# Row sums made row-major and transposed by the DMA, in an H3 convolution beside a Strassen feed-forward

## The chip, the cores and the metric

One Trainium2 chip, one NeuronCore of it. The metric is the device time of one execution in microseconds (us). The kernel before has a median of 1271.46 us over three runs.

## The reference

A gated H3 convolution and a feed-forward are added to x; shapes are S = 2048 rows, D = 1024 columns, F = 3584 hidden columns, all in float32.

```python
x = q                                     # 1 x 2048 x 1024
xn = layernorm(x)
k_shift = sum(k_pad[:, t:t + S] * shift_k[:, 3 - t] for t in range(4))
kv = k_shift * v
y = irfft(rfft(kv, 2 * S) * rfft(ssm_k, 2 * S))[:, :S] + kv * ssm_D   # a long causal convolution per channel
out = x + xn * y + silu(xn @ w1) @ w2
```

For this document the last term matters: the rows of x are layer-normed, multiplied by w1 (GEMM1), put through SiLU and multiplied by w2 (GEMM2). The convolution runs beside it as background work on VectorE and ScalarE, with some matmuls for its Fourier transforms, and is added into the same output.

## The kernel before, in words

**Precision.** Each operand is split into a high and a low float16 part (`split`, L357: the high part by an ACT copy, the low part by a DVE scalar_tensor_tensor). Each product is three matmuls, high by high, high by low, low by high: lines 917 to 919 in GEMM1 (`steps`, L912), 1047 to 1049 in GEMM2 (`steps2`, L1043). [...]

**Seven products.** Most of GEMM1 is done in units of seven products in place of eight (Strassen in Winograd's form, `PRODUCTS`, L39). x is cut into quarters A11, A12, A21, A22 and their sums S1 to S4; each product takes one of the seven x tiles (A11, S3, S2, A12, S1, S4, A22 for P1, P7, P6, P2, P5, P3, P4) and one factor of w1. `units` (L953) writes the order: P1, P7, P6, P2, P5, the next unit's P1, P3, P4. Three products share the bank `two`: `evacuate` (L880) copies P1 on ACT into it, P6 is added onto it, ACT copies that out, P5 is added, ACT copies it out, P3 is added. `seen["P1"]`, `seen["P6"]` and `seen["P5"]` are set by these ACT copies, `made[...]` by the products. P2 is added onto P1's own bank `one`. The first four units are plain (eight products, `plain_unit`, L922; they need A11 and A12 alone). Then come 26 units with seven products: 12 for the upper 1024 rows (sp = 0), then 14 for the lower 1024 rows (sp = 1).

**Where the x tiles come from.** Rows arrive in 16 blocks t of 128 rows (`load_row`, L463), are normed on DVE (`ln_rows`, L469, the last step at L506), and transposed on PE through an identity (`transposes`, L512, matmuls at L525): each block in two groups of four 128x128 float32 transposes, 128 in all, into PSUM. Blocks 0 to 3 give A11 and A12 (`first_rows`, L533), and ACT keeps a copy of their transposes (`keep`, L548). Blocks 4 to 7 give A21 and A22; `lower_sums` (L575) and `upper_sums` (L590) make S1 to S4 from the transposed tiles on DVE (v_tt, L336), ACT copying A21 out of PSUM for it. All results are split into tiles of 128 x 4 x 4 x 2 x 128 float16, one megabyte each, in `places`. For sp = 1 (blocks 8 to 15) the same is done in background, with the split parts stored to DRAM (`spill`, L648, 28 stores of 256 KB into xspA and xspS). `load_x` (L990) brings the seven tiles back, one plain DMA of 1 MB each, as each place comes free: a place is free after its product in the last unit of sp = 0.

**Order of the work.** All engines run instruction lists that a planner writes at build time (`Order`, L106). Every stream of work is a Python generator with a bias; the planner takes the operation that can start first by its own costs (`V`, `A`, `T`, `L`, `X`, `G`, L313 to L331), less the bias. SP issues plain DMAs (L, L324) and DMA transposes (X, L329); the planner counts 0.4 and 0.6 us of SP for them and the same transfer time per byte for both. POOL issues the accumulating stores into `out` (G, L333). What the planner wrote is fixed: on the chip each engine takes its list in order and waits where it must. The existing DMA transposes are those of the convolution, hl<-cm, 128x1024 float16, 32 in all.

**GEMM2.** Plain row blocks t take five chunks of W2 each; `TOGETHER` (L1040) says which blocks share a pass over the chunks at its start, so that a chunk is used by several blocks before the next is needed. While a chunk is made, spare PSUM banks (`ff`) go to the convolution. Then `units2` (L1065) does seven-product units for the rest, with `evacuate2` (L1112) writing to `out`; in the last unit the quarter (1, 0) is not accumulated by POOL but loaded from `out` (hf<-out), added on DVE and stored by SP. "conv out" is the flag that the convolution's stores are issued.

**The convolution's end.** `rest` makes the gated result yt by DVE in tiles of its own ring or of `hts`, and POOL adds it to `out` once `copies` (L1186) has written x into that part of `out`.

Of the kernel before, what the change touches and what calls it, by code (L numbers as in the profile page):

```python
# [20 lines left out]
P = 128  # L21
# [267 lines left out]
def h3_ffn_kernel(ctx, tc, x, kp, vs, fs, shift, dskip, w1, w2, cfwd, cinv, out):  # L289
# [123 lines left out]
    sums_r = Ring(order, lnp, "s", 4)  # L413
    s1_r = Ring(order, lnp, "s1", 4)
    xst_r = Ring(order, lnp, "xst", 3)
# [47 lines left out]
    def load_row(t):  # L463
        yield xts_r.ready
        xts[t] = xns[t] = xts_r.tile([P, D], uses=6 if t < 4 else 2)
        yield L(xts[t][0], xr[t // T2, t % T2])
        flag["xt", t].set()

    def ln_rows():  # L469
        for t0, n, bias in ((0, 2, 0.26), (2, 2, 0.17), (4, 4, 0.15), (8, 8, 0.03)):  # L470
# [33 lines left out]
            for t in order_in:  # L504
                xt, i = xts[t][0], slice(t - t0, t - t0 + 1)
                yield V(lambda: nc.vector.tensor_scalar(xt, xt, m[:, 0, i], rstd[:, t:t + 1], op0=ADD, op1=MUL),  # L506
                        xt, [xt, m[:, 0, i], rstd[:, t:t + 1]], us=0.78)
                flag["xn", t].set()
# [3 lines left out]
    def transposes():  # L512
        jobs = [(t, a) for t in range(4) for a in range(2)]
        jobs += [(4 + i, a) for i in range(4) for a in range(2)]
        for i in range(4):
            jobs += [(12 + i, 0), (12 + i, 1), (8 + i, 0), (8 + i, 1)]
        for t, a in jobs:
            yield flag["xn", t]
            xn, tok = xns[t]
            yield ft.ready  # L520
            pt, ptok = ft.tile([P, KH, P], uses=2)

            def mm():
                for c in range(KH):
                    nc.tensor.transpose(pt[:, c, :], xn[:, (KH * a + c) * P:(KH * a + c + 1) * P], ident)  # L525
            yield T(mm, pt, [xn], 0.5, m=0.3)
            tok.set()
            pts.append((pt, ptok))
# [4 lines left out]
    def first_rows():  # L533
        for n, name in enumerate(("A11", "A12")):
            xo[0][name], xtok[0][name] = places[XPLACE[name]].tile([P, 4, KH, 2, P], F16)
        for t in range(4):
            two = []
            for name in ("A11", "A12"):
                yield next_pt
                two.append(pts.pop(0))  # L540
                pt, tok = two[-1]
                o = xo[0][name]
                add(split(o[:, t, :, 0], o[:, t, :, 1], pt, XS, (tok, flag["rows", t], flag["x", 0, name])), 0.2)
            add(keep(t, two), 0.19)

    kept = {}

    def keep(t, two):  # L548

        xt, xtk = xts[t]  # L550
        kept[t] = []
        for a, (pt, tok) in enumerate(two):
            o = xt[:, a * W:(a + 1) * W].rearrange("p (k w) -> p k w", k=KH)
            yield a_act(o, pt, AF.Copy)
            tok.set()
            kept[t].append((o, xtk))
        flag["kept", t].set()

    def next_sum(ring, uses):
        yield ring.ready  # L560
        return ring.tile([P, KH, P], uses=uses)

    def next_transposed():
        yield next_pt
        return pts.pop(0)

    def give(to, name, src, tok):

        put = to(name)
        if put is None:  # L570
            tok.set()
        else:
            add(put(src, tok), to.bias)

    def lower_sums(to, ring):  # L575

        a21, k21 = yield from next_transposed()
        c21, kc = yield from next_sum(sums_r, 1)
        yield a_act(c21, a21, AF.Copy)
        k21.set()  # L580
        give(to, "A21", a21, k21)
        a22, k22 = yield from next_transposed()
        s1, ks1 = yield from next_sum(ring, 2)
        yield v_tt(s1, a22, c21, ADD)
        k22.set()
        give(to, "A22", a22, k22)
        give(to, "S1", s1, ks1)
        return c21, kc, s1, ks1

    def upper_sums(to, ring, c21, kc, s1, ks1, t=None):  # L590

        if t is not None:
            yield flag["kept", t]
        a11, k11 = kept[t][0] if t is not None else (yield from next_transposed())
        s2, ks2 = yield from next_sum(ring, 2)
        yield v_tt(s2, s1, a11, SUB)
        ks1.set()
        give(to, "S2", s2, ks2)
        yield v_tt(c21, a11, c21, SUB)
        k11.set()  # L600
        give(to, "A11", a11, k11)
        give(to, "S3", c21, kc)
        a12, k12 = kept[t][1] if t is not None else (yield from next_transposed())
        s4, ks4 = yield from next_sum(ring, 1)
        yield v_tt(s4, a12, s2, SUB)
        ks2.set()
        k12.set()
        give(to, "A12", a12, k12)
        give(to, "S4", s4, ks4)

    second = {}

    def x_rows():
        yield from first_rows()
        second["A21"], second["tok"] = places[4].tile([P, 4, KH, 2, P], F16)
        for name in ("A22", "S2", "S3", "S1", "S4"):
# [4 lines left out]
        class Kept:  # L621
            bias = 0.14

            def __init__(self, i):
                self.i = i

            def __call__(self, name):
                if name in ("A11", "A12"):
                    return None
                o = (second["A21"] if name == "A21" else xo[0][name])[:, self.i]  # L630
                return lambda src, tok: split(o[:, :, 0], o[:, :, 1], src, XS, (tok, flag["x", 0, name]))

        yield 0.14
        half = []
        for i in range(4):
            half.append((yield from lower_sums(Kept(i), s1_r)))
        Kept.bias = 0.11
        yield 0.11
        for i in range(4):
            yield from upper_sums(Kept(i), xst_r, *half[i], t=i)  # L640

        class Spilled(Kept):
            bias = 0.02

            def __call__(self, name):
                return None if name == "A21" else lambda src, tok: spill(xsp[name][:, self.i], src, tok)

        def spill(o, src, tok):  # L648
            yield lambda: s1_r.ready() or xst_r.ready()
            r = s1_r if s1_r.ready() else xst_r  # L650
            st, stok = r.tile([P, KH, 2, P], F16)
            yield from split(st[:, :, 0], st[:, :, 1], src, XS, (tok,))
            yield L(o, st)
            stok.set()
            flag["spilled"].set()

        yield 0.02
        for i in range(4):
            part = yield from lower_sums(Spilled(i), sums_r)
            yield from upper_sums(Spilled(i), sums_r, *part)  # L660
        flag["x done"].set()

# [290 lines left out]
    def units():  # L953
# [5 lines left out]
        for n, (i, sp) in enumerate(todo):  # L959
# [8 lines left out]
            add(evacuate(i, 2 * sp, one, c, made, seen), EB)  # L968
            yield from product("P7", i, sp, c[0], True)
# [70 lines left out]
    TOGETHER = ([range(2)] + [(t,) for t in range(2, NT)],  # L1040
# [71 lines left out]
    def evacuate2(u, one, c, made, seen):  # L1112
# [16 lines left out]
        a, at_ = vs_r.tile([P, W])  # L1129
        yield made["P6"]  # L1130
# [13 lines left out]
        if last:  # L1144
            yield flag["conv out"]
            yield hfs.ready
            o, otok = hfs.tile([P, W])
            yield L(o, at(u, 1, 0))
# [12 lines left out]
    flag["conv out"] = Token(NG * 4 * 2)  # L1161
# [9 lines left out]
    def load_h():  # L1171
# [7 lines left out]
        for u, n in uses2():  # L1179
# [4 lines left out]
            flag["h2", u, n].set()  # L1184

    def copies():  # L1186
        n = NT // 2
        for a in range(NT):
            yield flag["unit", a // 2] if a < n else flag["result", a - n]
# [134 lines left out]
    def convolution(floor):  # L1324
# [368 lines left out]
        def gated(g, t, py, tok):  # L1693
# [3 lines left out]
            yield lambda: r.ready() or flag["quads", 1]() and hts.ready()  # L1697
            yt, ytok = (r if r.ready() else hts).tile([P, 2, 2, P], uses=2)
# [8 lines left out]
            for b in range(2):  # L1707
                yield G(out4[b][:, :, t, g * P:(g + 1) * P], yt[:, b])
                ytok.set()
                flag["conv out"].set()  # L1710
# [25 lines left out]
    def more_rows():  # L1736
        for t in (8, 9, 12, 13, 10, 11, 14, 15):
            yield from load_row(t)
        yield L(taps, shift)
        yield L(cfw, cfwd)  # L1740
        yield L(civ, cinv)

    def more_pairs():
        for n in range(2, len(pairs)):
            yield from load_pair(n)
            if n == 3:
                add(load_factors_late(), 0.05)

# [69 lines left out]
```

## Time and profile before

| | |
|---|---|
| median of three runs | 1271.46 us (1269.89 to 1276.68) |
| profiled execution: time, span | 1272.2 us, 1270.4 us |
| granted PE clock, mean | 0.992 |
| first GEMM matmul (L917) starts | 14.8 us |
| GEMM1 ends, GEMM2 begins | 595.7, 601.8 us |
| last GEMM matmul starts | 1259.83 us |
| packets, those under 512 B | 253894, 48752 |

How to read it. The page groups instructions by source line, engine, operation and tile names with the buffer numbers left out. A group row ends in its busy time and mean length (ns), then the idle time before it and what released it. A timeline row is start, length, engine, line, operation. A 128x512 matmul shows 0.38 us from its first to its last element, but the next one starts 0.215 us after it: matmuls overlap, and what counts is the distance between starts. DMA shares are those of 16 engines; a share at or over 1 means that they were full. "q" behind an engine's name is its queue: SPq rows are DMA issues, and their length is how long the issue held SP.

### The profile page before, as it was taken

The numbers are of one execution on the slowest core, as the hardware profiler recorded it, in microseconds if no ns is written. First come the engines' busy times: TensorE is split into PE (matmuls) and PEld (weight loads), VectorE is DVE, ScalarE is ACT, GpSimd is POOL, SyncE is SP. The second block draws the span as 40 slices with busy tenths as digits, with TensorE's granted clock in tenths as the row PEclk, the third lists the DMA queues.
The fourth block names the chain that finished last, engine by engine and source line by source line (L and its number), as shares of the span: only waits on it lengthen the run. The fifth ranks groups of instructions, "written<-read, shape, count | busy, mean of one in ns | idle before, by whom it ended". The sixth has DMA issues, their size and how long they took to land.

```text
span 1270.4 us, 17081 instructions
## 1 busy us (share of the span) xinstructions
PE 1234.8 (97%) x6018; PEld 595.6 (47%) x6018; DVE 1150.0 (91%) x1533; ACT 734.2 (58%) x1169; POOL 132.9 (10%) x141
## 2 busy tenths in 40 slices
PE   7899999999999999999999999999999999999996
PEld 6444544444444444444344544444454454445443
DVE  8999998899599969999999799989979989998995
ACT  6857887778766686657654542473263245535232
POOL 0000000000000030001210210120030021113213
PEclk9899999999999999999999999999999999999998
DMA  9447799979999798879998786599577668978766
GB/s 331 158 141 241 261 319 317 299 254 353 299 362 286 236 272 284 239 218 260 334 367 212 166 243 142 138 254 268 126 163 214 140 150 243 259 151 152 158 121 92
DMA packets 253894, 292.94 MB, mean 231 GB/s; under 512 B 48752, under 2 KB 167536, under 8 KB 251632
## 3 DMA queue, kind: packets, MB, share of 16 engines
q1 hardware_dynamic: 227072, 266.93, 66.7%
q0 software_dynamic: 26736, 24.92, 15.0%
q8 instruction: 47, 0.77, 0.2%
q14 instruction: 39, 0.32, 0.1%
HBM read 193.22 MB, written 98.57 MB: 230 GB/s over the span
## 4 chain that ended last, share of the span: by engine, by line
PE 24%; DVE 19%; issue 8%; DMA 6%; ACT 2%; POOL 2%; SPq 0%; POOLq 0%; DVEq 0%; ACTq 0%
DVE spec L336 7%; PE ff L1048 7%; PE ff L1047 7%; PE ff L1049 7%; DVE tmp L336 3%; POOL out L333 2%; DVE ht L339 1%; DMA hf<-in_w 1%; DVE x L339 1%; DVE acc L339 1%; DMA kin<-in_kp 1%; DVE spec L339 1%; DMA out<-yt 1%; PE ps L1493 1%; PE ps L1495 1%
## 5 line engine op out<-in xcount | busy, mean ns | idle before, releaser
L1047 PE MATMUL ff<-x,wo 128*128 128x512 f16 x864 | 327.9, 380 | 2.7 <-ACT x L347 1.6
L1048 PE MATMUL ff<-x,wo 128*128 128x512 f16 x864 | 328.1, 380 | 1.3 <-DVE x L339 1.3
L1049 PE MATMUL ff<-x,wo 128*128 128x512 f16 x864 | 328.0, 380 | 0.0
L917 PE MATMUL ff<-x,wo 128*128 128x512 f16 (+1 forms) x808 | 304.6, 377 | 3.5 <-ACT hf L347 3.4
L918 PE MATMUL ff<-x,wo 128*128 128x512 f16 (+1 forms) x808 | 304.4, 377 | 2.5 <-DVE x L339 2.5
L919 PE MATMUL ff<-x,wo 128*128 128x512 f16 (+1 forms) x808 | 304.4, 377 | 0.4 <-DVE wo L339 0.4
L336 DVE TENSOR_TENSOR spec<-spec 128x512 f32<-128x512 f32 (+2 forms) x256 | 261.0, 1054 | 2.3
L1049 PEld LDWEIGHTS <-wo 128*128 128x128 f16 x864 | 84.6, 98 | 103.8 <-issue 2.1
L1048 PEld LDWEIGHTS <-wo 128*128 128x128 f16 x864 | 84.6, 98 | 103.5 <-issue 4.6
L1047 PEld LDWEIGHTS <-wo 128*128 128x128 f16 x864 | 85.6, 99 | 100.3 <-issue 0.6
L919 PEld LDWEIGHTS <-wo 128*128 128x128 f16 x808 | 79.4, 98 | 96.9 <-issue 4.1
L918 PEld LDWEIGHTS <-wo 128*128 128x128 f16 x808 | 79.5, 98 | 92.3 <-issue 5.7
L917 PEld LDWEIGHTS <-wo 128*128 128x128 f16 x808 | 80.9, 100 | 87.9 <-issue 1.1
L333 POOL DMA_DIRECT2D out<-yt x64 | 72.4, 1300 | 344.0 <-DVE yt L339 204.3
L347 ACT ACTIVATE hf<-ff,invc 128x512 f32<-128x512 f32 x64 | 43.7, 684 | 111.7 <-PE ff L1049 87.7
L333 POOL DMA_DIRECT2D out<-hf x63 | 56.6, 898 | 459.6 <-ACT hf L347 400.1
L336 DVE TENSOR_TENSOR tmp<-spec 128x2048 f32<-128x2048 f32 (+1 forms) x48 | 92.6, 1935 | 1.1
L347 ACT ACTIVATE spec<-spec 128x1024 bf16<-128x1024 f32 x32 | 33.8, 1058 | 89.3 <-DVE spec L336 89.3
L339 DVE SCALAR_TENSOR_TENSOR acc<-kin,taps,acc 128x1024 f32<-128x1024 f32 x48 | 61.6, 1283 | 15.0 <-ACT acc L347 14.4
L339 DVE SCALAR_TENSOR_TENSOR ht<-hf,wsc,ht 128x1024 f16<-128x1024 f32 (+1 forms) x56 | 67.4, 1204 | 6.7 <-ACT ht L347 6.6
L347 ACT ACTIVATE ht<-hf,wsc 128x1024 f16<-128x1024 f32 (+1 forms) x56 | 61.0, 1089 | 10.8 <-DMA hsfS<-ht 4.1
L347 ACT ACTIVATE spec<-ps 128x512 f32<-128x512 f32 x92 | 52.9, 590 | 17.3 <-PE ps L1495 14.3
(175 smaller groups left out, 1744.2 us busy)
## 6 DMA issues: line engine op xcount, KB each, us to landing
wo<-hs SPq DMA_DIRECT2D x160, 256.0 KB, 3.5
hs<-ht SPq DMA_DIRECT2D x80, 256.0 KB, 4.5
out<-hf POOLq DMA_DIRECT2D x63, 256.0 KB, 4.3
wraw<-in_w SPq DMA_DIRECT2D x31, 512.0 KB, 5.9
raw<-in_w SPq DMA_DIRECT2D x28, 512.0 KB, 5.8
kin<-in_kp SPq DMA_DIRECT2D x16, 704.0 KB, 6.0
xt<-in_x SPq DMA_DIRECT2D x16, 512.0 KB, 7.3
kf<-in_fs SPq DMA_DIRECT2D x8, 1024.0 KB, 5.6
```

The source lines that it names most:

```text
L333: return Op("POOL", 1.1, 3.0, lambda: nc.gpsimd.dma_start(o, i, accum_op=ADD), [i], [o], m, n)
L336: return V(lambda: nc.vector.tensor_tensor(o, a, b, op=op), o, [a, b], **k)
L339: return V(lambda: nc.vector.scalar_tensor_tensor(o, a, s, b, op0=op0, op1=op1), o, [a, b] + ([] if isinstance(s, float) else [s]), **k)
L347: nc.scalar.activation(o, i, func, scale=scale, **kw)
L917: nc.tensor.matmul(o, w[:, 0, k], xf[:, :, k, 0], start=first and k == 0, stop=False, **kw)
L918: nc.tensor.matmul(o, w[:, 0, k], xf[:, :, k, 1], start=False, stop=False, **kw)
L919: nc.tensor.matmul(o, w[:, 1, k], xf[:, :, k, 0], start=False, stop=last and k == KH - 1, **kw)
L1047: nc.tensor.matmul(po, hx[:, n, 0, :], wc[:, n, 0, :], start=first and n == 0, stop=False, **kw)
L1048: nc.tensor.matmul(po, hx[:, n, 0, :], wc[:, n, 1, :], start=False, stop=False, **kw)
L1049: nc.tensor.matmul(po, hx[:, n, 1, :], wc[:, n, 0, :], start=False, stop=last and n == 3, **kw)
L1493: nc.tensor.matmul(o, cf[:, 0], hi[i], start=i == 0, stop=False, **kw)
L1495: nc.tensor.matmul(o, cf[:, 1], hi[i], start=False, stop=True, **kw)
```

## The change

1. Blocks 8 to 15 are no longer transposed on PE; `transposes` has 16 groups in place of 32. The sums are made row-major on DVE, in place, on the normed rows (`low_sums`, `up_sums`; as many 128x512 operations as before), and split row-major into new tiles `s`. For sp = 0, S1 to S4 are brought into the x tiles by 16 DMA transposes of 256 KB from SBUF. For sp = 1 the split parts are stored row-major, and `load_x` reads them back by seven DMA transposes of 1 MB from DRAM. ACT's copies of kept transposes and of A21 are gone.
2. The last step of the layer norm of blocks 4 to 7 is done by ACT (Identity with scale and bias) and not by DVE.
3. The first seven-product unit has the order P1, P2, P7, P6, next P1, P5, P3, P4. P2 waits there for the ACT copy of P1; P3 stands directly behind P5.
4. In GEMM2 three row blocks share the first pass over W2's chunks, where two did.
5. The load of hf<-out in the last unit stands ahead of the copy after P6, "conv out" counts only the first half of the column groups, and yt may take tiles of `wo` once the hidden tiles are loaded.
6. The copies of x into the second half of `out` are issued four results later; three constants (taps, cfw, civ) are loaded after the sixth weight pair and not after the rows.

```diff
-        for t, a in jobs:
+        for t, a in [(t, a) for t in range(8) for a in range(2)]:
...
+                if n == 4:
+                    yield a_act(xt, xt, AF.Identity, rstd[:, t:t + 1], nmr[:, t:t + 1])
...
+    def row_parts(sp, i, names, src, tok):
+        n = len(names)
+        yield sums_r.ready if n == 1 else sums_r.pairs
+        o, otok = (sums_r.tile if n == 1 else sums_r.pair)([P, n * KH, 2, P], F16, n)
+        yield from split(o[:, :, 0], o[:, :, 1], src.rearrange("p (k w) -> p k w", w=P), XS, (tok,))
+        for f, name in enumerate(names):
+            q = o[:, f * KH:(f + 1) * KH]
+            if sp == 0:
+                yield X(xo[0][name][:, i].rearrange("p k h w -> p (k h) w"), q.rearrange("p k h w -> p (k h w)"))
+                flag["x", 0, name].set()
+            else:
+                yield L(xsp[name][:, i], q)
+                flag["spilled"].set()
+            otok.set()
...
+    def low_sums(sp, i, bias):
+        x, y, z, v = quarters(sp, i)
+        low, tok = xns[8 * sp + 4 + i]
+        yield v_tt(v, z, v, ADD)
+        yield v_tt(z, x, z, SUB)
+        add(row_parts(sp, i, ("S3", "S1"), low, tok), bias)
+
+    def up_sums(sp, i, bias):
+        x, y, z, v = quarters(sp, i)
+        up, tok = xns[8 * sp + i]
+        yield v_tt(x, v, x, SUB)
+        xns[8 * sp + 4 + i][1].set()
+        yield v_tt(y, y, x, SUB)
+        add(row_parts(sp, i, ("S2", "S4"), up, tok), bias)
...
+            if n == 0:
+                yield seen["P1"]
+                yield from product("P2", i, sp, one[0])
+                made["P2"].set()
             yield from product("P7", i, sp, c[0], True)
...
-            yield from product("P2", i, sp, one[0])
-            made["P2"].set()
-            yield seen["P6"]
-            yield from product("P5", i, sp, two)
-            made["P5"].set()
+            if n > 0:
+                yield from product("P2", i, sp, one[0])
+                made["P2"].set()
+                yield seen["P6"]
+                yield from product("P5", i, sp, two)
+                made["P5"].set()
...
+            if n == 0:
+                yield seen["P6"]
+                yield from product("P5", i, sp, two)
+                made["P5"].set()
...
-            yield L(xo[1][name], xsp[name])
+            yield X(xo[1][name].rearrange("p i k h w -> p (i k h) w"), xsp[name].rearrange("p i k h w -> p (i k h w)"))
...
-    TOGETHER = ([range(2)] + [(t,) for t in range(2, NT)],
+    TOGETHER = ([range(3)] + [(t,) for t in range(3, NT)],
...
-    flag["conv out"] = Token(NG * 4 * 2)
+    flag["conv out"] = Token(NG // 2 * 4 * 2)
...
-            yield lambda: r.ready() or flag["quads", 1]() and hts.ready()
-            yt, ytok = (r if r.ready() else hts).tile([P, 2, 2, P], uses=2)
+            yield lambda: r.ready() or flag["quads", 1]() and hts.ready() or flag["h end"]() and wo.ready()
+            r = wo if flag["h end"]() and wo.ready() else r if r.ready() else hts
+            yt, ytok = r.tile([P, 2, 2, P], uses=2)
```

More of the change, by code (lines that the diff above doesn't have):

```diff
@@ L520, in transposes @@
             yield ft.ready
-            pt, ptok = ft.tile([P, KH, P], uses=2)
+            pt, ptok = ft.tile([P, KH, P])
             def mm():
@@ L536, in first_rows @@
         for t in range(4):
-            two = []
             for name in ("A11", "A12"):
                 yield next_pt
-                two.append(pts.pop(0))
-                pt, tok = two[-1]
+                pt, tok = pts.pop(0)
                 o = xo[0][name]
                 add(split(o[:, t, :, 0], o[:, t, :, 1], pt, XS, (tok, flag["rows", t], flag["x", 0, name])), 0.2)
[L544 to L609, printed above, removed]
     second = {}
@@ L619, in x_rows @@
             xo[0][name], xtok[0][name] = r.tile([P, 4, KH, 2, P], F16)
[L621 to L631, printed above, removed]
         yield 0.14
-        half = []
+        none = Token()
@@ L635, in x_rows @@
         for i in range(4):
-            half.append((yield from lower_sums(Kept(i), s1_r)))
-        Kept.bias = 0.11
+            for name in ("A21", "A22"):
+                yield next_pt
+                pt, tok = pts.pop(0)
+                o = xo[0][name][:, i]
+                add(split(o[:, :, 0], o[:, :, 1], pt, XS, (tok, flag["x", 0, name])), 0.14)
         yield 0.11
         for i in range(4):
[L640 to L655, printed above, removed]
+            yield from low_sums(0, i, 0.13)
+        for i in range(4):
+            yield from up_sums(0, i, 0.11)
         yield 0.02
         for i in range(4):
-            part = yield from lower_sums(Spilled(i), sums_r)
-            yield from upper_sums(Spilled(i), sums_r, *part)
@@ L1129, in evacuate2 @@
         a, at_ = vs_r.tile([P, W])
+        if last:
+            yield flag["conv out"]
+            yield hfs.ready
+            o, otok = hfs.tile([P, W])
+            yield L(o, at(u, 1, 0))
         yield made["P6"]
@@ L1144, in evacuate2 @@
         if last:
[L1145 to L1148, printed above, removed]
             yield v_tt(a, a, o, ADD)
@@ L1184, in load_h @@
             flag["h2", u, n].set()
+        flag["h end"].set()
     def copies():
```

37 lines of the change are left out of this document (22 added, 15 removed).

## The prediction

> **What bounds the kernel now.** I read the page first, the engine shares and the idle times of the matmul groups, then the table by stage.
>
> ```profile
> PE 1234.8 (97%) x6018; PEld 595.6 (47%) x6018; DVE 1150.0 (91%) x1533; ACT 734.2 (58%) x1169; POOL 132.9 (10%) x141
> L1047 PE MATMUL ff<-x,wo 128*128 128x512 f16 x864 | 327.9, 380 | 2.7 <-ACT x L347 1.6
> L1048 PE MATMUL ff<-x,wo 128*128 128x512 f16 x864 | 328.1, 380 | 1.3 <-DVE x L339 1.3
> L917 PE MATMUL ff<-x,wo 128*128 128x512 f16 (+1 forms) x808 | 304.6, 377 | 3.5 <-ACT hf L347 3.4
> ```
>
> PE is busy for 97% of the span, and its three lines of each GEMM hardly wait. So the time is what PE has to issue, plus a few stalls, plus the ends. Next, the windows: length, then busy time of PE, PEld, DVE, ACT and POOL, granted clock, DMA share, GB/s.
>
> ```profile
> 80.00:100.00 20.00, 20.00 (x96) 9.24 (x95) 19.11 (x42) 12.68 (x18) 0.00 (x0) 1.00 0.61 198
> 100.00:120.00 20.00, 20.00 (x96) 9.23 (x95) 18.61 (x43) 16.97 (x23) 0.00 (x0) 1.00 0.76 244
> 160.00:180.00 20.00, 19.93 (x101) 9.85 (x100) 19.44 (x33) 16.87 (x28) 0.00 (x0) 1.00 0.95 320
> 280.00:330.00 50.00, 50.00 (x233) 22.66 (x232) 42.78 (x62) 37.37 (x55) 0.00 (x0) 1.00 1.04 333
> 330.00:440.00 110.00, 108.47 (x507) 49.41 (x505) 100.36 (x115) 74.36 (x117) 0.76 (x1) 1.00 0.95 305
> ```
>
> Two things are to be seen. PE is full in every one of these stages, so a matmul taken out is worth its issue time there. And the DMA engines are full from 280 to 440, where the second row half's x tiles come in, at 333 GB/s, while they have a quarter to a third free at 80 to 120. A DMA that gets slower is free in the one place and not in the other.
>
> **The change part by part**, against the profiled run (span 1270.4, run 1272.2; the median is 1271.46, so 0.7 comes off at the end).
>
> *64 PE transposes go* (rows 8 to 15: 16 groups of four).
>
> ```profile
> 181.88 0.38 PE L918 MATMUL ff<-x,wo 128*128 128x512 f16 x1
> 182.10 0.38 PE L919 MATMUL ff<-x,wo 128*128 128x512 f16 x1
> 182.37 0.66 PE L525 MATMUL ft<-ident,xt 128*128 128x128 f32 x4
> 182.87 0.38 PE L917 MATMUL ff<-x,wo 128*128 128x512 f16 x1
> L347 ACT ACTIVATE s<-ft 128x512 f32<-128x512 f32 x8 | 4.7, 583 | 0.0
> ```
>
> From the L919 to the next L917 is 0.77 us with the group between them; without it, two neighbours stand some 0.215 apart (181.88 and 182.10). A group costs 0.55 and 16 cost 8.8. DVE keeps its 32 sums and nearly all splits, ACT loses 16 copies, eight of them those of the last row (0.58 us each). Bounds: all 8.8, or nothing, if DVE (19.44 of 20 at 160 to 180) is what PE would wait for next. I take **-8.8**, since PE is the fuller of the two and DVE's work there gets no longer.
>
> *The first unit's order* (P1, P2, P7, P6, P1, P5, P3, P4).
>
> ```profile
> 83.67 0.38 PE L919 MATMUL ff<-x,wo 128*128 128x512 f16 x1
> 84.08 0.60 ACT L347 ACTIVATE hf<-ff 128x512 f32<-128x512 f32 x1 [1.50 <-PE ff L919]
> L506 DVE TENSOR_SCALAR xt<-xt,mv,rstd 128x1024 f32<-128x1024 f32 x16 | 12.3, 810 | 0.0
> L347 ACT ACTIVATE x<-wraw,tau 128x1024 f16<-128x1024 f32 x10 | 11.5, 1147 | 2.6 <-DMA wraw<-in_w 2.6
> ```
>
> These first two rows are the copy of P1's bank. P2 adds onto that bank, so PE now waits until 84.68 plus a handover, where its next matmul stood at 83.89: 0.9. P3 behind P5 waits for the next such copy, 0.9 again; what stands behind these matmuls on PE is the whole stream, so both count in full. In return P7 and P6, whose S3 and S2 now come through the DMA, are asked for 12 matmuls later. Sixteen transposes of 256 KB are issued by SP meanwhile, in the stages with the free DMA share. Rows 4 to 7 are normalized on ACT (1.15 each, by the last row, of the same size) and not in 0.81 on DVE: four times 0.34, of which I let 0.5 reach PE. Bounds -1 (nothing waits, since the sums come no later) and +5 (the last S2 lands late). I take **+2.3**.
>
> *The seven x tiles of the second half come by DMA transposes of 1 MB.* No row of before has that size or a DRAM source; the nearest is hl<-cm, 128x1024 in two bytes, 0.26 MB.
>
> ```profile
> L329 SPq DMA_TRANSPOSE hl<-cm x31: 1231/1287/6640, 291.8 to 1159.7; - x31
> DMA to landing us min/median/max: 3.0/4.1/10.5
> 781.70:783.00 1.30, 1.30 (x7) 0.58 (x6) 1.26 (x2) 0.00 (x0) 0.00 (x0) 1.00 1.13 201
> x<-xspS SPq DMA_DIRECT2D x4, 1024.0 KB, 7.6
> x<-xspA SPq DMA_DIRECT2D x3, 1024.0 KB, 8.3
> ```
>
> In the window 781.70 to 783.00 one such transpose has the DMA engines to itself (issued at 780.48): they are full, and move 201 GB/s. The stage of the x loads ran at 333, with the engines full too. So 1.05 MB takes 5.2 us as a transpose and 3.15 as a copy; SP's median of 1.287 us for a quarter of it says the same (5.1). Now the place where it happens:
>
> ```profile
> 283.73 1.79 SPq L324 DMA_DIRECT2D x<-xspA  x1
> 290.72 0.94 SPq L324 DMA_DIRECT2D x<-xspS  x1
> 291.75 3.60 SPq L329 DMA_TRANSPOSE hl<-cm  x1
> 301.78 6.64 SPq L329 DMA_TRANSPOSE hl<-cm  x1
> 309.14 0.38 SPq L324 DMA_DIRECT2D x<-xspA  x1
> 298.30 0.38 PE L917 MATMUL ff<-x,wo 128*128 128x512 f16 x1
> 328.13 0.38 PE L917 MATMUL ff<-x,wo 128*128 128x512 f16 x1
> ```
>
> The first load (A11) can be issued at 283.73, when its place comes free, the last (A22) at 309.14. By the program's order PE first reads A11 at 298.30 and A22 at 328.13. Between them SP issues, in the changed order, seven x tiles (7.34 MB), three transposes hl<-cm (0.79 MB) and 6.03 MB of copies: pieces of W1's factors, of the hidden tiles, two raw pieces and one kf. At the two speeds: 36.5 + 3.9 + 18.1 = 58.5 us, and with a backlog of up to 4 us at 283.73 (an estimate: 8.3 to land, less 3.15 of its own and about 1 of latency) the last lands at 342.2 to 346.2 where PE wants it at 328.13, **14 to 18 us late**. That was 3.15 a tile: 48.0 with the backlog, some 4 late. I take 16. PE spends it in several waits in front of the S2, A12, S1, S4 and A22 products, and such waits have a second price in this trace, which the next fence shows: about 1.5 for one period at half clock. So **+17.5**. Bounds: 0, if all of it goes at copy speed and the copies give way, and +26, if transposes from DRAM go a quarter slower than that row (6.5 us each, an estimate) with a second half-clock period. The queue to suffer is SP's: every factor load stands behind an x tile of 5 us; I have not priced that, and keep it in the upper bound.
>
> [...]
>
> *Three row blocks share W2's chunks at the start of GEMM2, where two did.*
>
> ```profile
> 628.29 0.38 PE L1049 MATMUL ff<-x,wo 128*128 128x512 f16 x1
> 630.23 0.38 PE L1047 MATMUL ff<-x,wo 128*128 128x512 f16 x1 [1.56 <-ACT x L347]
> 631.86 0.58 PE L1048 MATMUL ff<-x,wo 128*128 128x512 f16 x1 [1.26 <-DVE x L339]
> 632.24 0.63 PE L1049 MATMUL ff<-x,wo 128*128 128x512 f16 x1
> 635.12 0.38 PE L1047 MATMUL ff<-x,wo 128*128 128x512 f16 x1
> ```
>
> The last of five chunks comes late: 1.94 and 1.63 between starts where 0.215 is the step, 3.1 us lost, and then, by the last three rows, eight more steps in 3.26 us where 1.72 would do, 1.5 lost: half clock. A chunk serves 12 matmuls for each block, 2.59 us; with a third block the fifth chunk is wanted four times 2.59 = 10.4 us later, less the few matmuls of the convolution that had the spare bank. It was 3.4 us late. I take **-4.6**, all of it; bounds -4.6 and 0 (the spare bank's work comes back as a wait later).
>
> [...]
>
> *The last unit's end.*
>
> ```profile
> 1259.83 0.38 PE L1049 MATMUL ff<-x,wo 128*128 128x512 f16 x1
> 1260.93 0.75 DVE L339 SCALAR_TENSOR_TENSOR yt<-ps,csc,ht 128x512 f32<-128x512 f32 x1 [1.97 <-DMA out<-yt]
> 1262.37 0.69 ACT L347 ACTIVATE hf<-ff,invc 128x512 f32<-128x512 f32 x1 [9.77 <-DVE hf L336]
> 1262.38 0.75 DVE L339 SCALAR_TENSOR_TENSOR hf<-ff,invc,hf 128x512 f32<-128x512 f32 x1
> 1263.73 1.50 POOL L333 DMA_DIRECT2D out<-hf  x1
> ```
>
> 10 us lie between PE's last GEMM matmul and the end. DVE stands behind yt, which waits for a buffer; the ACT copy of P3, ready 2.6 us before PE's end, stands behind DVE's sum of hf; and the last accumulating store goes out at 1263.73. With the sum moved ahead and yt given free wo tiles, DVE's last operation follows PE at about 1260.3 where it now starts at 1262.38, and POOL's last store can leave 2.5 us or more before 1263.73. **-3.5**, bounds -4.2 and -1 (POOL's queue, 1.1 us an issue, still ends last).
>
> The later constants and out copies cost nothing that I can see: their consumers are 100 us away.
>
> **Sum:** -8.8 + 2.3 + 17.5 - 4.6 - 3.5 = +2.9, so 1272.2 + 2.9 = 1275.1 for a profiled run; less 0.7, **1274**.
>
> **Rivals.**
> - *Transposes at copy speed.* The switch costs at most the 4 us by which the longer queue is late: 14.5 (seven times 2.07) less, with the half clock's 1.5 or without: 1274 - 14 = **1260**. For it: no row shows this size or a source in DRAM. Against: 201 GB/s.
> - *Transposes from DRAM slower than that row, and the backlog stays.* The engines were full until 440, so 19 us of additional transfer time can't be caught up soon: +26 for +17.5, and a few us of late factors: 1274 + 8 + 4 = **1286**. It decides from about 5.8 us a tile. For it: landings of up to 10.5 us and SP held for 6.64 at 301.78, both where the engines are full.
> - *DVE gets the transposes' 8.8.* DVE is at 19.44 of 20; if the factors come no sooner, the switch at 283 is reached as late as before: **1282**.
> - *The gains at the ends don't come* (the spare bank and POOL's queue): up to 6 us more, **1280**.
>
> **How the numbers follow.** Forecast 0.40, copy speed 0.25, slow transposes 0.20, DVE 0.08, the ends 0.07. A measurement of this kernel can tell about 0.5%, 6.4 us, from no change: faster is below 1265.1, slower above 1277.8. Faster takes the copy-speed case and a little of the forecast's own spread (1267 to 1281): 0.28. Slower takes slow transposes, most of DVE and the ends, and a third of the forecast: 0.40. Within: 0.32. The range reaches to the two main rivals: **1257 to 1290**.
>
> **What would show it.** A trace with 1 MB transposes landing every 5 us and PE waits for them at the start of the second half proves the main step; if they pass at 3 us, it was wrong, and the time is below 1265. Two waits on ACT of 0.9 in the first unit, no wait on x in the fifth chunk of GEMM2, no transposes behind the eighth row, and 6 to 7 us from the last matmul to the end answer to the other steps. New waits on DVE's wo between 140 and 280 would show the DVE rival, and idle PE at 330 to 440 the backlog.

## The result and the profile after

The changed kernel takes 1286.46 us (median of six runs, 1284.33 to 1288.58), the kernel before 1272.64 beside it (six runs, 1266.96 to 1276.68). The ratio is 1.0109, 95% interval 1.008 to 1.0138: 13.8 us slower, inside the range on record, 12 above the predicted 1274. The profiled execution has a span of 1285.4 us, 15.0 more than the one before.

The page of the changed kernel; its GEMM1 lines are now L864 to L866 and its GEMM2 lines L1003 to L1005.

```profile
PE 1233.1 (96%) x5954; PEld 589.1 (46%) x5954; DVE 1144.5 (89%) x1509; ACT 725.0 (56%) x1137; POOL 132.8 (10%) x141
DMA packets 298676, 297.11 MB, mean 231 GB/s; under 512 B 94432, under 2 KB 213216, under 8 KB 297312
L864 PE MATMUL ff<-x,wo 128*128 128x512 f16 (+1 forms) x808 | 305.9, 379 | 25.9 <-DVE hf L336 12.0
L1003 PE MATMUL ff<-x,wo 128*128 128x512 f16 x864 | 327.4, 379 | 1.5 <-ACT hf L347 0.9
```

The first GEMM1 line now waits 25.9 us (3.5 before), GEMM2 hardly at all. Packets under 512 B have nearly doubled: of the added 45680, 45056 are by count the 256 B pieces of the new transposes (16 x 1024 and 7 x 4096; one hl<-cm in the kernel before, from 781.65 to 783.05, shows 1056 packets for 0.27 MB).

Both programs issue the same number of GEMM matmuls, so the start of the n-th one, counted from 0, can be set side by side. The plain units have the first 240, so the stretch from 180 to 360 holds the first seven-product unit and the start of the next; 2460 is 36 matmuls into GEMM2. From the two traces, in us:

| from, to the n-th GEMM matmul | before, at | after, at | after - before in this stage | on record |
|---|---|---|---|---|
| start to 180 (plain units) | 63.16 | 61.67 | -1.5 | - |
| to 360 (first seven-product unit) | 102.15 | 111.00 | +10.3 | +2.3 |
| to 720 (transposes of rows 8 to 15 gone) | 188.83 | 189.25 | -8.4 | -8.8 |
| to 1440 (switch to the second half) | 357.02 | 380.70 | +23.3 | +17.5 |
| to 2460 (end of GEMM1) | 614.26 | 637.42 | -0.5 | - |
| to 2580 (W2's first pass) | 644.84 | 663.32 | -4.7 | -4.6 |
| to the last one | 1259.83 | 1277.60 | -0.7 | - |
| from it to the end of the span | 1270.43 | 1285.37 | -2.8 | -3.5 |

The stages add up to +15.0. Three of the five terms came out within 1 us of the forecast; the first unit and the switch carry the whole error.

**The first unit** of the changed kernel: one row of SP, one window, and the rows of PE and ACT that waited.

```profile
74.59 12.83 SPq L329 DMA_TRANSPOSE x<-s  x8
75.00:88.00 13.00, 7.72 (x36) 3.23 (x33) 12.65 (x31) 2.54 (x4) 0.00 (x0) 0.93 1.07 229
78.10 0.38 PE L864 MATMUL ff<-x,wo 128*128 128x512 f16 x1 [0.73 <-ACT ff L347]
88.11 0.58 PE L864 MATMUL ff<-x,wo 128*128 128x512 f16 x1 [4.67 <-DMA x<-s]
98.83 1.06 ACT L347 ACTIVATE junk<-raw 128x1024 bf16<-128x1024 f32 x1 [1.16 <-DMA raw<-in_w]
99.88 0.58 ACT L347 ACTIVATE hf<-ff 128x512 f32<-128x512 f32 x1
100.51 0.38 PE L864 MATMUL ff<-x,wo 128*128 128x512 f16 x1 [2.02 <-ACT hf L347]
```

The bubble in front of P2 (78.10) is the 0.9 of the forecast. But eight transposes follow one another on SP from 74.59 for 12.83 us, 1.6 us each, with the DMA engines full (1.07), and the last S2 piece comes when PE has stood 4.67 us in front of P6; P6's twelve matmuls then run at half clock (granted 0.50 from 88.11 to 93.00; 0.58 at the start, then 0.63, where 0.38 is the rule). The second bubble (100.51, in front of P3) is 2.0 and not 0.7: the ACT copy of the bank, at 99.88, stands behind an ACT operation on a raw piece of w1 (98.83), whose load stands behind the transposes on SP and was issued at 92.06.

**The switch.** SP's rows of the changed kernel:

```profile
299.75 7.37 SPq L329 DMA_TRANSPOSE x<-xspS  x1
307.21 1.26 SPq L329 DMA_TRANSPOSE hl<-cm  x1
308.56 4.84 SPq L329 DMA_TRANSPOSE x<-xspS  x1
314.12 5.17 SPq L329 DMA_TRANSPOSE x<-xspA  x1
319.38 5.47 SPq L329 DMA_TRANSPOSE x<-xspS  x1
328.32 6.38 SPq L329 DMA_TRANSPOSE x<-xspS  x1
335.98 5.53 SPq L329 DMA_TRANSPOSE x<-xspA  x1
```

And its waits: PE's from 280 to 370 (total, times, longest), ACT's from 300 to 360, and the two rows of the longest.

```profile
PE ff L864 <- DVE hf L336: 12.0, 1, 12.0
PE ff L864 <- ACT hf L347: 3.9, 1, 3.9
PE ps L1451 <- DMA hl<-cm: 3.3, 2, 3.1
```

```profile
ACT ht L347 <- DMA hsfA<-ht: 14.2, 4, 8.8
ACT ht L347 <- DMA hsfS<-ht: 6.1, 2, 3.7
```

```profile
350.88 1.15 ACT L347 ACTIVATE ht<-hf,wsc 128x1024 f16<-128x1024 f32 x1 [8.84 <-DMA hsfA<-ht]
355.51 0.58 PE L864 MATMUL ff<-x,wo 128*128 128x512 f16 x1 [11.95 <-DVE hf L336]
```

A tile holds SP 4.8 to 7.4 us, and the last one lands 7.5 us after its issue, at 343.5, as the forecast's 342 to 346 had it. What the forecast did not have is who waits: no row names x<-xsp. When PE comes to read them, the seven tiles have been there for 2.5 to 13 us, because something else has held PE up first. PE waits for the convolution's hl<-cm, issued behind a tile at 307.21; ACT waits 20.3 us (7.5 before) for buffers ht whose stores hsfA and hsfS stand behind tiles; and the 12 us at 355.51 are the end of such a chain. By the program order, DVE's sum of P7's bank has to write a tile that the splits into ht must read first. The ACT half of that split waited until 350.88; PE's P4 needs the bank. PE's three rows make 19.2 us, where it waited 1.5 before; a stretch at half clock follows each of the three long waits (granted 0.52 from 311.41, 0.50 from 332.01 and from 355.51) and makes up most of the rest.

**The tail**, PE's last GEMM matmul and what follows it.

```profile
1277.60 0.38 PE L1005 MATMUL ff<-x,wo 128*128 128x512 f16 x1
1277.91 1.73 POOL L333 DMA_DIRECT2D out<-hf  x1
1278.02 0.75 DVE L339 SCALAR_TENSOR_TENSOR hf<-ff,invc,hf 128x512 f32<-128x512 f32 x1 [3.16 <-PE ff L1005]
1278.80 0.34 SPq L324 DMA_DIRECT2D out<-hf  x1
```

DVE follows PE at once, and 7.8 us lie between the last matmul and the end where it was 10.6.

### The profile page after: what moved, and what is told of

The parts are those of the page before. It is cut to its first block, busy times and chain, and to the rows that moved or that the text cites. A ratio compares the mean times of both kernels' runs of the same rounds, so it can differ in the third digit from the quotient of the medians.

```text
span 1285.4 us, 16871 instructions
## 1 busy us (share of the span) xinstructions
PE 1233.1 (96%) x5954; PEld 589.1 (46%) x5954; DVE 1144.5 (89%) x1509; ACT 725.0 (56%) x1137; POOL 132.8 (10%) x141
## 4 chain that ended last, share of the span: by engine, by line
PE 51%; DVE 32%; DMA 8%; issue 4%; ACT 3%; SPq 1%; POOL 1%; POOLq 0%; DVEq 0%; ACTq 0%
DVE spec L336 10%; PE ff L864 8%; PE ff L865 8%; PE ff L866 8%; PE ff L1003 7%; PE ff L1004 7%; PE ff L1005 7%; DVE tmp L336 5%; DVE spec L339 2%; DVE ht L339 2%; DVE x L339 2%; DVE acc L339 1%; DMA xg<-in_x 1%; DVE st L480 1%; DMA wraw<-in_w 1%
## 5 line engine op out<-in xcount | busy, mean ns | idle before, releaser
L864 PE MATMUL ff<-x,wo 128*128 128x512 f16 (+1 forms) x808 | 305.9, 379 | 25.9 <-DVE hf L336 12.0
L1003 PE MATMUL ff<-x,wo 128*128 128x512 f16 x864 | 327.4, 379 | 1.5 <-ACT hf L347 0.9
L1005 PE MATMUL ff<-x,wo 128*128 128x512 f16 x864 | 327.4, 379 | 0.0
L866 PE MATMUL ff<-x,wo 128*128 128x512 f16 (+1 forms) x808 | 306.0, 379 | 1.6 <-DVE wo L339 1.4
L1005 PEld LDWEIGHTS <-wo 128*128 128x128 f16 x864 | 84.5, 98 | 102.0
L1003 PEld LDWEIGHTS <-wo 128*128 128x128 f16 x864 | 85.4, 99 | 99.7
L864 PEld LDWEIGHTS <-wo 128*128 128x128 f16 x808 | 81.4, 101 | 96.5 <-issue 8.7
L866 PEld LDWEIGHTS <-wo 128*128 128x128 f16 x808 | 79.6, 99 | 99.0 <-issue 5.2
L333 POOL DMA_DIRECT2D out<-yt x56 | 62.1, 1297 | 332.5 <-DVE yt L339 315.5
```

Of the source, the lines that this page charges most:

```text
L333: return Op("POOL", 1.1, 3.0, lambda: nc.gpsimd.dma_start(o, i, accum_op=ADD), [i], [o], m, n)
L864: nc.tensor.matmul(o, w[:, 0, k], xf[:, :, k, 0], start=first and k == 0, stop=False, **kw)
L866: nc.tensor.matmul(o, w[:, 1, k], xf[:, :, k, 0], start=False, stop=last and k == KH - 1, **kw)
L1003: nc.tensor.matmul(po, hx[:, n, 0, :], wc[:, n, 0, :], start=first and n == 0, stop=False, **kw)
L1005: nc.tensor.matmul(po, hx[:, n, 1, :], wc[:, n, 0, :], start=False, stop=last and n == 3, **kw)
```

## The experiments

All ratios are to the kernel before, run beside the experiment; the changed kernel's is 1.0109. Theory A: what PE waits for at the switch is what stands behind the x tiles on SP's in-order queue. Theory B, the prediction's: the x tiles arrive after their products want them. Where a run below reads x tiles by copies in place of transposes, or by transposes where they were stored transposed, these tiles hold their numbers in the wrong order, and only its time is of use.

**Copies for transposes at the switch, in the changed order.**

```diff
-            yield X(xo[1][name].rearrange(...), xsp[name].rearrange(...))
+            o, s = xo[1][name], xsp[name]
+            yield Op("SP", 0.6, 0.1, lambda: nc.sync.dma_start(o, s), [s], [o], 0.3, size(o) * P * 2)
```

> The changed kernel with the seven 1 MB x tiles of the second row half read back by plain copies in the planned order of the transposes (same planner cost), so that the second half's x tiles hold untransposed data; everything else is as changed. The changed kernel loses 25 us to PE gaps between 307 and 359 us. If the transposes cause all of that, by whatever way, those gaps fall to 0 to 4 us and the time to 1286.5 - 23 = 1262 to 1266. If it is another part (the order of the background work, DVE), the gaps stay and the time is above 1275.

1274.17 against 1269.19 (ratio 1.0045, 1.0026 to 1.0065): some 8 us less than the changed kernel by the ratios (11.6 between the two profiled spans), and not 20 to 24. In both traces every engine does its work in the same order. PE's only long wait at the switch:

```profile
PE ff L864 <- DVE hf L336: 9.1, 1, 9.1
```

From the 1140th to the 1440th GEMM matmul this kernel loses 9.1 us against before, the changed one 23.1. So transposes cost 14 there and the order of the work 9; a few us of the 14 are lost again elsewhere. With the tiles in time, DVE's sum for P7's bank still stands behind convolution operations (some 5 us of them) and two splits, which the planner put there.

**The transposes alone, in the order of before.**

```diff
-            yield L(xo[1][name], xsp[name])
+            o, s = xo[1][name].rearrange(...), xsp[name].rearrange(...)
+            yield Op("SP", 0.4, 0.1, lambda: nc.sync.dma_start(o, s, transpose=True), [s], [o], 0.3, 2 ** 20)
```

> One part alone: the kernel before in its own order, only the seven x tiles of the second half are read by DMA transposes instead of copies (they were stored transposed already, so the second half's x tiles hold the wrong arrangement). The prediction's step (later landing alone, 14 to 18 us with half clock 17.5) gives 1269 + 14 to 18 = 1283 to 1287. If the changed order of the background work carries part of the 25 us, as e1_plain's remaining 9.5 us gap says, this one shows about 13 to 15: 1282 to 1284. If speed hardly matters, below 1275.

1286.19 against 1270.21 (1.0131, 1.01 to 1.0162): +16.0, and between those two matmuls +16.7, with every engine's order that of before. The longest of its PE waits from 280 to 370, a window with hardly anything but x tiles moving, and two rows of the chain:

```profile
PE ps L1494 <- DMA hl<-cm: 11.7, 3, 5.8
301.20:317.30 16.10, 13.26 (x62) 5.85 (x60) 10.21 (x15) 10.33 (x15) 0.00 (x0) 1.00 1.02 205
318.48 1.42 SPq L329 DMA_TRANSPOSE hl<-cm  x1
322.74 0.58 PE L1494 MATMUL ps<-hl,cfw 128*128 128x512 f16 x1 [4.29 <-DMA hl<-cm]
```

From DRAM, with rows of 8 KB, transposes move 205 GB/s, the 201 of the SBUF ones in the prediction. PE stands in front of a matmul of the background, L1494, which the list puts between two GEMM matmuls and whose operand was issued behind two x tiles. No x tile is waited for. The wait is on SP and not in the transfer: once issued, these hl<-cm land in 4.1 to 6.4 us, where they took 5.9 to 10.5 before. Whether a tile holds SP because it is being issued or because the DMA engines are full, these runs don't tell apart: both last as long. Theory A holds here. The size is that of the forecast, but not for its reason, as the last tile's issue and landing show:

```profile
324.95 5.26 SPq L997 DMA_TRANSPOSE x<-xspA  x1
x<-xspA SPq DMA_TRANSPOSE x1, 7.3
```

It lands at 332.2, only 4 us behind the 328.13 at which PE read it in the kernel before. By that, lateness alone would have cost some 4 us (an estimate), not 16.

**Three tiles in place of seven**, the same edit for A11, A12 and A22 only.

> The kernel before in its own order, with DMA transposes for the x tiles A11, A12 and A22 alone and copies for the four S tiles (wrong arrangement in three tiles). e7_xload lost 16 us with seven. If the loss comes from bytes and lateness of the tiles: three cost 3 x 2.07 = 6.2 us of transfer against 10 us of room (the last tile landed 10 us ahead of its product), so 0 to 2 us, 1270 to 1272. If it comes from what stands on SP behind them (each holds SP 4.4 us longer, and hl<-cm stands right behind A12's): some 4 to 8 us, 1274 to 1278.

1276.64 against 1270.99 (1.0049, 1.0032 to 1.0065): +5.7. Bytes and lateness gave 0 to 2. SP, and PE's wait:

```profile
309.21 4.86 SPq L329 DMA_TRANSPOSE hl<-cm  x1
314.79 7.24 SPq L998 DMA_TRANSPOSE x<-xspA  x1
328.68 3.18 SPq L329 DMA_TRANSPOSE hl<-cm  x1
```

```profile
PE ps L1497 <- DMA hl<-cm: 5.9, 2, 5.4
```

The same wait again, half as long. Theory B falls for the order of before; in the changed kernel it has against it that PE's waits name no x tile.

**The planner told the price** (in the changed kernel).

```diff
-        return Op("SP", 0.6, 0.1, lambda: nc.sync.dma_start(o, i, transpose=True), [i], [o], m, n)
+        return Op("SP", 1.3 * n / 262144, 0.1, lambda: nc.sync.dma_start(o, i, transpose=True), [i], [o], m, n * 333 / 201)
```

> The changed kernel, where only the planner's price of a DMA transpose is set to the measured one: SP held 1.3 us for 256 KB and a transfer at 201 GB/s. Theory A (SP's in-order queue: the x transposes hold SP for 5.2 us each, the stores of the hidden tiles stand behind them, ACT and DVE wait for those buffers and PE for ACT and DVE): a planner that knows this puts the stores ahead, and about half of the 25 us come back, 1272 to 1278, in the first unit too. Theory B (the x tiles themselves arrive late, a matter of bytes and speed): the same transfers have to end before the same products, 1283 to 1288.

1283.00 against 1269.19 (1.0107, 1.0071 to 1.0142): no gain, as theory B had it. PE's waits from 280 to 370:

```profile
PE ff L864 <- DVE hf L336: 9.5, 1, 9.5
PE ff L864 <- DMA x<-xspS: 6.3, 2, 4.7
```

**The tiles cut in four as well**, with that price.

```diff
-            yield X(xo[1][name].rearrange(...), xsp[name].rearrange(...))
+            for k in range(4):
+                yield X(xo[1][name][:, k].rearrange(...), xsp[name][:, k].rearrange(...))
```

> The changed kernel with each 1 MB x transpose of the second half cut into four of 256 KB, and the planner's price of a transpose set to the measured 1.3 us of SP and 201 GB/s, so that small transfers can pass between the quarters. Bytes and speed of the x tiles are the same. Theory A (what waits is everything that stands behind a tile on SP): the waits for ht buffers and hl<-cm shrink, the gaps between 300 and 360 fall from 25 to about 10 us, 1268 to 1274. Theory B (the tiles come too late): the gaps stay at 15 to 20, with DMA x<-xsp as the releaser, 1278 to 1284.

1290.27 against 1270.21 (1.0167, 1.0142 to 1.0192): slower than either theory gave.

```profile
PE ff L866 <- DMA x<-xspA: 5.6, 1, 5.6
PE ff L866 <- DMA x<-xspS: 5.3, 2, 3.8
PE ff L866 <- DVE hf L336: 4.1, 1, 4.1
```

In these two no PE wait for hl<-cm is left, and now the tiles are late. So theory A alone doesn't lead to a cure: between the issue of A11 and the read of A22 in the kernel before lie 44 us, of which the seven tiles take 37 by the forecast's rate (an estimate), and the planner can only choose who waits. The lateness which the prediction worked out is there for the changed order (343.5 against the 328.13 of before); in the changed kernel the transfers behind paid for it, in these two the tiles.

**Stores from another queue**: the hidden tiles' stores hsfA and hsfS issued by POOL.

```diff
-                yield L(hsf[sp][name][:, :, PAIRS.index(i)]..., ht[:, 4 * f:4 * f + 4]...)
+                yield Op("POOL", 1.1, 3.0, lambda: nc.gpsimd.dma_start(to, src), [src], [to], 0.3, size(src) * P * 2)
```

> The changed kernel with the stores of the seven-product hidden tiles (hsfA and hsfS <- ht) issued by POOL and not by SP. Theory A: ACT's 20 us of waits for those buffers between 300 and 360 go, with the 12 us PE wait at 343; the tiles themselves landed at 343 where PE would want the last one at about 333, so 10 us stay: 1271 to 1277. Theory B: the tiles land as late as before, nothing is gained, 1284 to 1288.

1301.86 against 1269.19 (1.0255, 1.0215 to 1.0294). ACT's waits for ht between 280 and 370 fell to 3.4 us as theory A said, but the planner's order changed with the prices, ACT now stood 14.3 us behind hl<-cm, and PE 15.5 behind the same DVE sum and 8.0 for x tiles. As a test between the theories it is inconclusive.

**The first unit: S1 to S4 by copies**, in the same order.

```diff
-                yield X(xo[0][name][:, i].rearrange(...), q.rearrange(...))
+                to = xo[0][name][:, i]
+                yield Op("SP", 0.6, 0.1, lambda: nc.sync.dma_start(to, q), [q], [to], 0.3, 2 ** 18)
```

> The changed kernel with the sixteen 256 KB transposes of S1 to S4 of the first half replaced by plain copies in the same order at the same planner price, so that these four x tiles hold untransposed data. If the transposes' speed (1.3 us each of SP and DMA, 16 in 31 us) is what makes P6 wait at 83, the 4.8 us wait, its half-clock period (1.6 to 2.6) and the raw piece that stands behind them on SP (1.5 of the gap at 98) go: 8 us faster than the changed kernel, with 0.9 left at each of the two bank copies. If DVE's sums are what is late, 2 us or less.

1276.88 against 1270.21 (1.0061, 1.0035 to 1.0087): about 6 us less than the changed kernel, and its PE waits from 60 to 140 are only these:

```profile
PE ff L865 <- ACT ff L347: 0.7, 1, 0.7
PE ff L865 <- ACT hf L347: 0.7, 1, 0.7
```

The stretch takes +1.8 against before (40.75 us from the 180th to the 360th matmul, 38.99 before), where the forecast had 2.3. All else in the first unit is the speed of the sixteen transposes.

**The first unit's order undone.** The edit takes the `n == 0` branches out again.

> The changed kernel with the first unit in the usual order P1, P7, P6, P2, P5. The last S2 transpose lands at 88 whatever the order; P6 would now be wanted at 79.4 and not at 83.1, so PE waits some 8.7 in one piece in place of 0.9 + 4.8, and P5 and P3 have the next P1 between them (the 2.2 gap goes). Sum: about 1 us slower to 1 us faster than the changed kernel. If P2's place matters more (the idle time in one piece costs another half-clock period), 3 us slower.

1299.36 against 1270.21 (1.0235, 1.0195 to 1.0276). In the first unit it is as expected: one wait of 8.1, and +10.8 for the unit where the changed kernel has +10.3. The rest, some 13 us, is lost far behind it, mostly from 600 us on; PE's waits there:

```profile
PE ps L1442 <- ACT tmp L347: 3.8, 2, 1.9
PE ps L1442 <- ACT spec L347: 3.2, 1, 3.2
PE ps L1634 <- DVE yt L339: 3.2, 1, 3.2
```

They are the background's matmuls (ps). An edit of one unit made the planner write another order for the whole kernel.

**The parts at the ends alone**, on the kernel before: three blocks on W2's first pass, the last unit's load, yt in wo, later copies.

> The kernel before with only the parts at the ends: three row blocks on the first pass over W2, the last unit's load moved ahead, yt in free wo tiles, out copies later. By the terms of the sum (-4.6 and, as the changed kernel's trace has it, -2.8) 1272.6 - 7 = 1265. If the spare bank's work comes back as waits, or the W2 gain needs the later start of GEMM2 that the changed kernel has, 1269 to 1273.

1272.98 against 1269.19 (1.0036, 1.0012 to 1.006): no gain. Its profiled execution took 1268.63, near the lowest of its ten runs, and PE's last GEMM matmul starts 8.9 us earlier there than before. Of these 8.9, 2.4 stand already at the 2460th matmul, ahead of which every engine's order is that of before: they are the spread between two runs. But the convolution now ends last:

```profile
1250.93 0.38 PE L1049 MATMUL ff<-x,wo 128*128 128x512 f16 x1
1257.81 0.74 DVE L339 SCALAR_TENSOR_TENSOR wo<-ps,csc,ht 128x512 f32<-128x512 f32 x1
1261.94 1.11 POOL L333 DMA_DIRECT2D out<-wo  x1 [0.27 <-issue]
```

The inverse transforms stand behind the last GEMM matmul, and 15.9 us follow it. Why the median lies 4 us over the profiled run stays open.

**W2's first pass alone**, on the kernel before.

```diff
-    TOGETHER = ([range(2)] + [(t,) for t in range(2, NT)],
+    TOGETHER = ([range(3)] + [(t,) for t in range(3, NT)],
```

> The kernel before with nothing but three row blocks on the first pass over W2's chunks. In two traces (the changed kernel and e2_ends) this step was worth 4.7 us of PE time at 615 to 640. If that is kept to the end: 1270 - 4.7 = 1265. If the planner's new order of everything behind it (an order that differs by chance, as in e4_order, which lost 12 us far from its edit) decides: 1268 to 1275.

1273.58 against 1270.99 (1.0021, 1.0002 to 1.004). The stall is gone (PE is 4.7 us further ahead from 614 to 640), and given back: 2.0 at 700 to 740 to the convolution's yt, 2.6 at 1102, where PE waits once for ACT (2.06 us in front of 1102.74), and 5.7 at the end, where 16.3 us follow the last GEMM matmul. PE's waits from 640 on:

```profile
PE ff L1047 <- ACT hf L347: 2.8, 2, 2.1
PE ps L1493 <- DVE yt L339: 2.4, 2, 2.2
```

**A version made of the parts that gained**: sp = 0 as before, the second half's sums row-major, each piece transposed from SBUF to a staging tile and stored from there, x tiles by copies, three blocks on W2.

```diff
+            st, stok = stage_r.tile([P, KH, 2, P], F16)
+            yield X(st.rearrange(...), q.rearrange(...))
+            otok.set()
+            yield L(xsp[name][:, i], st)
```

> A version that keeps what was shown to gain and leaves out what lost: the kernel before with its PE transposes and sums for the first half and its plain x loads, the second half's sums row-major, each split piece transposed by a 256 KB DMA from SBUF to a staging tile as soon as it is made and stored from there (28 transposes from 130 to 260 us, priced 1.3 us in the planner), and three row blocks on W2's first pass. If the background stage takes the 28 x 1.3 = 36 us of SP and DMA time without PE noticing: 1270 - 8.8 - 4.7 = 1257. If they make the factors or the hidden tiles late there (the DMA engines are at 0.95 between 140 and 200): 1265 to 1280.

1408.51 against 1270.99 (1.1081, 1.1055 to 1.1107). PE is 9.3 us ahead at the 720th matmul, as the missing transposes promise, and loses far more at the switch:

```profile
PE ff L941 <- DMA x<-xspA: 82.6, 1, 82.6
PE ps L438 <- ACT spec L347: 36.2, 1, 36.2
```

There is one staging tile only; each piece passes through it in turn, transpose and store (SP waited 36.6 us for it), and in the background the last store was issued at 364.8 us, where the x tiles are wanted from 298. The convolution starts only after that, and PE waits for it again at the end. No version was found that beats the kernel before.

## Why the prediction was right, and where it was not

The range held, and of the three cases the likeliest (slower, 0.40) came; the forecast itself, 1274, was 12 us too low. That the range held is in part luck: the upper end was set by the rival of slower transposes, which the measured rate refutes, and other losses reached the same place.

- *64 PE transposes, -8.8*: right, -8.4 in the changed kernel, and -8.4 again in the kernel with copies for S1 to S4. The rival that DVE takes it fell.
- *The first unit, +2.3*: mis-sized, +10.3. Two bubbles of 0.9 were right (e9_splain; its 1.8 leaves nothing for the 0.5 of the layer norm), though the row at 84.08 that was read as P1's copy is P6's: 276 GEMM matmuls stand ahead of it, and P1's copy writes a bank (ff<-ff). It takes 0.58 us in the changed kernel, so the size did not suffer. The failed step is "in the stages with the free DMA share": the share at 80 to 120 was that of before, while the sixteen transposes are issued from 56.6 to 86.1, mostly ahead of that window, and fill the engines themselves: from 60 to 80 the share is 0.26 before and 1.05 after. Each holds SP for 1.35 us at the median, up to 3.3. The upper bound named the late S2 at +5, without the half clock that follows (2.5) and without the raw piece behind it (1.3).
- *The switch, +17.5*: the speed was right (200 to 205 GB/s for 1 MB from DRAM, 201 forecast). The sum of the queue fits the changed order: the last tile lands at 343.5 with transposes (forecast 342 to 346) and at 329.0 with copies (e1_plain; forecast 332). No run shows the "about 1 of latency" in its backlog of 4: in the kernel before, a 256 KB piece of hs lands 2.3 us after its issue at the least, of which 0.8 is transfer at 333 GB/s, and hl<-cm 3.0, of which 1.3 is transfer at 201, so 1.5 and 1.7 are left. The sum doesn't fit the kernel before, for which it gave "some 4 late": there the last tile, issued at 309.14, lands 8.3 us later, 10.7 us ahead of its product. So it is luck that the transposes alone, in the order of before, cost 16.0 (e7_xload), the forecast's number: the last tile comes 4 us late there by the schedule of before, and the loss is that of hl<-cm. The failed step is "PE spends it in several waits in front of the S2, A12, S1, S4 and A22 products" and "I have not priced that": the waits were for what stands behind the tiles, and not for the factor loads alone that the prediction kept in its upper bound. The other 9 us belong to the order that the planner wrote for the changed kernel; the prediction had no term for it. Shown by e1_plain is that they stay without transposes; that they are DVE's order is read from the program and the trace, not tried.
- *W2, -4.6*: right, -4.7 in the changed kernel and in e2_ends and e8_w2. The changed kernel keeps it to the end; alone it brought nothing (e8_w2).
- *The tail, -3.5*: -2.8 in the changed kernel. It isn't a property of the edit: e2_ends makes the same edit and has a tail of 15.9.
- *The rival of copy speed* (0.25) is refuted: no run shows a transpose at the 333 GB/s of the copies, and those of 1 MB moved 200 in the changed kernel and 205 in e7_xload. *The slow-transpose rival* came nearest in time, 1286, for another reason: the transposes were not slower than the row, but more was behind them.

## What to carry to other kernels

Price a DMA by what it does to its issuing queue, not only by its landing: in e7_xload PE waited 11.7 us for hl<-cm, a background transfer that stood behind x tiles on SP and whose consumer the static list puts into the main stream, and for no x tile. When a planner writes the whole order, an edit's gain read from one stage is an estimate until the whole is run, since 5 to 13 us moved elsewhere here with edits of a few lines. A free share of a resource is only free for as much as the change doesn't itself add: the DMA share from 60 to 80 us was 0.26 before and 1.05 after.

## What the runs showed of the hardware

A DMA transpose of float16 kept SP about as long as its transfer takes at the rates below, or longer: 1.23 us and up for 0.26 MB (hl<-cm in the kernel before; 1.30 at 201 GB/s) and 4.8 to 7.4 for 1.05 MB (x<-xsp in the changed kernel; 5.2 at 201), where the seven copies of 1 MB in the kernel before kept SP 0.3 to 1.8. With the 16 DMA engines full (shares of 1.01 to 1.13) the rate was 196 to 201 GB/s from SBUF, in pieces of 0.26 MB (the kernel before, from 781.70, 886.74 and 1160.90), and 200 and 205 from DRAM, in pieces of 1.05 MB (the changed kernel from 308.6 to 324.8, e7_xload from 301.2 to 317.3); the stage of the copies ran at 333 (the kernel before, 280 to 330). In the changed kernel half clock (granted 0.50 to 0.52) followed PE's waits of 3.08, 3.85, 4.67 and 11.95 us at 311.19, 331.15, 88.11 and 355.51, and in the kernel before the two of 1.56 and 1.26 that end at 630.23 and 631.86 (0.52); after the 2.02 at 100.51 in the changed kernel the clock stayed full (1.00 from 100.5 to 104). Its stretches at half clock from 88.11, 311.41 and 355.51 cost 2.5, 1.7 and 1.9 us.
